# Scheduling by engine clocks, low parts inside P, and a two-pass V in a fused attention and feed-forward kernel

## The chip, the cores and the metric

The kernel runs on one core of a Trainium2 chip. The metric is device time in microseconds (us) of one execution; lower is better. Engines are named as in the profile: PE (TensorE, matrix products), DVE (VectorE), ACT (ScalarE, Exp and Tanh), POOL (GpSimd) and SP (SyncE, which issues most transfers).

## The reference

Multi-query attention (32 heads of 16, one shared K and V) and a SiLU feed-forward block on the same 2048 x 512 input, mixed per row by a sigmoid gate. All in fp32.

```python
def _A_ref(x, wq, wk, wv, wo):                   # S = 2048, D = 512, H = 32, Dh = 16
    q = (x @ wq) -> heads;  k = x @ wk;  v = x @ wv
    p = softmax(einsum("bhqd,bkd->bhqk", q, k) * Dh ** -0.5)
    return einsum("bhqk,bkd->bhqd", p, v) -> rows @ wo
def _B_ref(x, w1, w2):                           # F = 1792
    return silu(x @ w1) @ w2
g = sigmoid((x * gate_w).sum(-1))
out = g * _A_ref(x) + (1 - g) * _B_ref(x)
```

## The kernel before

**Precision.** An fp32 operand is written as two fp16 parts, high and low, and a product is three fp16 products (high by high, high by low, low by high). Only P V is different, see below.

**A prologue** (up to some 39 us) loads and transposes x, makes K and V of all keys, and the queries of the first heads. V lies as VF (fp32), VH and VL (its fp16 high and low parts), per block of 128 keys a tile of 16 columns of V and a 17th of ones, which gives the row sums of P, padded to 32 columns. `v_parts` makes VH and VL.

**The loop** of `attention` goes over 32 rounds (4 chunks of 512 rows, 4 groups of 8 heads, two halves `rb`) of 16 steps (blocks of 128 keys). A step has two score groups. Everything PE does is cut into *slots*: eight matmuls on 64 x 32 (or 50 x 32) tiles of the array, 512 columns each, which run side by side.

- `scores(p)`: one slot gives a 128 x 1024 score tile S in PSUM (two such tiles), then one Exp on ACT writes half of a step's P (128 x 2048, fp32, four buffers). 1024 of these.
- `pv(s, n)`: P V of a step adds into two PSUM banks that collect a round. A *native* step multiplies fp32 P by VF: eight fp32 matmuls, which take four slots of time. A *split* step uses the upper 16 bits of P as bf16 (`upper`, every other half word) and the rest as fp16: `low` subtracts the upper half from P on DVE, in two operations of 1024 elements, into a tile L of its own. Then three slots: VH by upper, VL by upper, VH by L. Odd steps are native, even ones split unless `split_step` says otherwise. The first matmul of a step needs the Exps; only the third slot needs L.
- the *stream* (`outs`, `stream`): the products of the feed-forward block, the query projection and the output projection, each an `Out` with 6 or 12 terms. A stream slot holds a term of one output on the upper 64 rows of the array and a term of the output before it on the lower 64. `ffn_h` evicts with Tanh on ACT, a gate product on DVE (L790) and a split of H into two fp16 parts on DVE (`split_v`, L120 and L121); `ffn_o` and `out_proj` add into the output rows on DVE (`add_out`, L720 and L722); `q_block` writes queries out to DRAM. PSUM has two banks (`pm`) for the stream.
- closing a round (`norm_a`, L943 to L950): two transposes out of PSUM, a sum over 17 of every 32 columns, reciprocal and product; every second round a transpose and a split (`norm_b`, `norm_c`) that give O for the output projection.
- splitting raw weights (`Pieces.step`, 36 pieces, loaded through POOL's queue) and the maxima for a range check (`chores`) fill DVE.

**What sets the order.** It is written out by hand: two steps form a cycle, and a string gives its slots, S for scores, F stream, P split slot, N native step, B a bound for the queries. Longer strings take over when the stream is behind. DVE's optional work goes through `put` and `fill`, which fills a cycle up to an assumed length (3.7, 4.1 or 4.95 us).

```python
SPLIT, NATIVE = "SFFFSFFFSPPPSBN", "SFFFSFFFSNBSN"
            fill(4.95 if n_f > 6 else 4.1 if ended[0] and ended[0].hidden else 3.7)
```

When the scores are through, the stream's remaining outputs are made as *whole* products (`whole`, 128 x 128 x 512, one slot each), in order.

**Range check.** Maxima are compared with `RANGES` at the end; outside them, a second, slower pass with measured scales runs (`second_pass`). Both passes call `attention`.

## Time and profile before

| | us |
|---|---|
| median of 3 runs | 1079.93 |
| fastest | 1078.13 |
| slowest | 1380.04 |
| span of the profiled execution (first to last instruction) | 1075.3 |
| first Exp of the loop starts | 39.3 |
| last Exp of the loop starts | 1053.0 |
| granted TensorE clock, mean over the span | 0.998 of full |

The profiled execution's own time is not listed beyond its span; what lies around the span is the difference to the times above. In the views, busy time is the union of an engine's records, a duration in ns is the mean of one instruction, "x8" counts instructions merged into a row, "PEld" is the loading of weights into the array, and `out<-in` names what an instruction writes and reads. A "chain" view follows the last instruction back through what released it. A few per cent of the matmul records are missing from the trace, so a row of 24 may show as x23.

### The profile page before, as it was taken

Reading aid. Unit: us, or ns where it says so; the run is one execution under the profiler, and the core shown is the slowest. Engines: PE = TensorE matmul, PEld = TensorE weight load, DVE = VectorE, ACT = ScalarE, POOL = GpSimd, SP = SyncE. Lnnn points to the kernel's source line nnn. Section 1 sums busy time; section 2 is a strip of 40 time slices with the busy share of each in tenths; the row PEclk is TensorE's granted clock in tenths of the full one; section 3 lists DMA queues with packets and bytes.
Section 4 is the critical chain, followed back from the end, with each engine's and each line's share of the span. In section 5 each row is a group of like instructions: output and inputs, shape, how many; then the busy total and the mean of one; then the engine's idle time right before and its main releaser. Section 6 shows DMA issues by size and latency. Waiting matters only on the chain.

```text
span 1075.3 us, 65967 instructions
## 1 busy us (share of the span) xinstructions
PE 1057.2 (98%) x31224; PEld 667.5 (62%) x31224; DVE 789.9 (73%) x1082; ACT 1008.6 (94%) x1121; POOL 23.4 (2%) x53
## 2 busy tenths in 40 slices
PE   8999999999999999999999999999999999999996
PEld 5455776766665577677655568677756555555552
DVE  6856986968778786878777697675857767476875
ACT  5799999999999999999999999899989999999992
POOL 2110000000000000000000000000000000000000
PEclk9999999999999999999999999999999999999999
DMA  5311111220001000000000100000000110000001
GB/s 208 115 61 45 49 42 31 61 60 14 11 11 41 32 22 10 17 12 12 22 11 21 37 19 21 22 12 11 20 6 12 31 31 12 11 11 5 11 4 43
DMA packets 20840, 32.95 MB, mean 31 GB/s; under 512 B 5137, under 2 KB 12050, under 8 KB 20562
## 3 DMA queue, kind: packets, MB, share of 16 engines
q1 hardware_dynamic: 17618, 20.46, 5.9%
q0 software_dynamic: 2512, 8.13, 2.6%
q8 instruction: 246, 4.03, 1.5%
q14 instruction: 32, 0.26, 0.1%
q10 hardware_dynamic: 432, 0.07, 0.0%
HBM read 20.12 MB, written 8.52 MB: 27 GB/s over the span
## 4 chain that ended last, share of the span: by engine, by line
PE 89%; DVE 5%; ACT 4%; issue 1%; POOL 0%; POOLq 0%; ACTq 0%
PE pv L1043 35%; PE pm L741 31%; PE S L997 19%; ACT P L1000 4%; DVE L L1021 1%; PE pm L745 1%; PE pt L311 0%; PE pk L126 0%; DVE xs L117 0%; DVE T L943 0%; PE pk L127 0%; PE pk L125 0%; DVE U L944 0%; PE pm L342 0%; DVE T L945 0%
## 5 line engine op out<-in xcount | busy, mean ns | idle before, releaser
L1000 ACT ACTIVATE P<-S 128x1024 f32<-128x1024 f32 x1024 | 963.5, 1051 | 24.6 <-PE S L997 19.4
L997 PE MATMUL S<-qb,KT 50*32 50x512 f16 x8192 | 480.1, 378 | 2.3 <-ACT P L1000 2.2
L1021 DVE TENSOR_TENSOR L<-P 128x1024 f16<-128x1024 f32 x348 | 408.1, 1217 | 8.3 <-ACT P L1000 8.2
L1043 PE MATMUL pv<-P,VF 64*32 64x512 f32 x5408 | 374.8, 589 | 0.0
L997 PEld LDWEIGHTS <-KT 50*32 50x32 f16 x8192 | 188.6, 90 | 193.9 <-issue 126.7
L741 PE MATMUL pm<-w2s,H 64*32 64x512 f16 x5232 | 258.8, 375 | 0.6 <-DVE qx L825 0.2
L741 PE MATMUL pm<-xs,w1s 64*32 64x512 f16 x5376 | 248.5, 375 | 1.1 <-issue 0.6
L741 PEld LDWEIGHTS <-H 64*32 64x32 f16 x5232 | 143.7, 93 | 43.5 <-issue 11.3
L741 PEld LDWEIGHTS <-w1s 64*32 64x32 f16 x5376 | 136.3, 93 | 46.1 <-issue 13.5
L1043 PEld LDWEIGHTS pv<-P,VF 64*32 64x32 f32 x5408 | 125.0, 107 | 30.3 <-issue 8.1
L790 DVE SCALAR_TENSOR_TENSOR e<-e,pm 128x512 f32<-128x512 f32 x56 | 38.5, 687 | 140.3 <-ACT e L789 139.4
L1043 PE MATMUL pv<-P,VH 64*32 64x512 bf16 x1392 | 81.9, 389 | 0.0
L1043 PE MATMUL pv<-L,VH 64*32 64x512 f16 x1392 | 81.4, 374 | 0.0
L1043 PE MATMUL pv<-P,VL 64*32 64x512 bf16 x1392 | 81.4, 385 | 0.0
L741 PE MATMUL pm<-xs,wqs 64*32 64x512 f16 x1152 | 81.1, 375 | 0.0
L1043 PEld LDWEIGHTS <-VH 64*32 64x32 f16 x2784 | 60.7, 92 | 20.4 <-issue 3.8
L741 PE MATMUL pm<-wo_s,O 64*32 64x512 f16 x1440 | 63.3, 375 | 0.0
L943 DVE STREAM_TRANSPOSE T<-pv 128x512 f32<-128x512 f32 x32 | 23.0, 717 | 48.0 <-PE pv L1043 40.4
L722 DVE SCALAR_TENSOR_TENSOR acc<-pm,g,acc 128x512 f32<-128x512 f32 x48 | 35.8, 745 | 26.4 <-PE pm L741 24.6
L741 PEld LDWEIGHTS <-wqs 64*32 64x32 f16 x1152 | 43.6, 93 | 10.1 <-issue 2.8
L121 DVE TENSOR_TENSOR H<-e,H 128x512 f16<-128x512 f32 x56 | 38.8, 693 | 1.9
L789 ACT ACTIVATE e<-pm 128x512 f32<-128x512 f32 x56 | 34.5, 616 | 5.7 <-PE pm L741 5.7
(155 smaller groups left out, 478.9 us busy)
## 6 DMA issues: line engine op xcount, KB each, us to landing
qb<-qd SPq DMA_DIRECT2D x192, 32.0 KB
raw<-in_B_w_dram POOLq DMA_DIRECT2D x23, 256.0 KB, 2.9
xn<-in_A_x_dram SPq DMA_DIRECT2D x8, 512.0 KB
out_dram<-acc SPq DMA_DIRECT2D x16, 256.0 KB
qd<-qx SPq DMA_DIRECT2D x12, 256.0 KB
raw<-in_A_wo_dram POOLq DMA_DIRECT2D x4, 256.0 KB, 3.6
qb<-sh SPq DMA_DIRECT2D x62, 2.0 KB
raw<-in_B_w_dram SPq DMA_DIRECT2D x3, 256.0 KB
```

The source lines that it names most:

```text
L121: nc.vector.tensor_tensor(a2, a, a1, op=OP.subtract)
L722: nc.vector.scalar_tensor_tensor(a, po, gate[:, n:n + 1], a, op0=OP.mult, op1=OP.add)
L741: nc.tensor.matmul(self.bank[32 * m:32 * m + 32], l(i, rows, 32 * m), r(j, rows), start=first, stop=last)
L745: nc.tensor.matmul(self.bank, l(i, slice(0, 128), 0, 128), r(j, slice(0, 128)), start=first, stop=last)
L789: nc.scalar.activation(e, ph, AF.Tanh, scale=t_scale)
L790: nc.vector.scalar_tensor_tensor(e, e, 1.0, ph, op0=OP.add, op1=OP.mult)
L943: nc.vector.transpose(T, pv[0])
L997: nc.tensor.matmul(sc[32 * m:32 * m + 32, f], KT[b:b + 50, k0:k0 + 32], qtile[i][b:b + 50, j], start=True, stop=True)
L1000: nc.scalar.activation(P[:, 2 * j:2 * j + 2], sc, AF.Exp, scale=scale_of(c, o))
L1021: nc.vector.tensor_tensor(lows[s][:, q], P[:, q], upper(P)[:, q], op=OP.subtract)
L1043: nc.tensor.matmul(pvs[i][h][32 * j:32 * j + 32], a[r], b[r, j], start=first, stop=last)
```

## The change

The strings and the cycle filler go. The program now keeps three clocks while it writes instructions out, `pe`, `act` and `dve`, with a fixed duration for each kind of work, and picks the next slot by them: a score when the one before the last should be through Exp, else stream or P V as far as they are ready by the clocks. DVE's operations become tasks with a duration, a time from which they are ready and a due time; `serve` issues them up to PE's clock.

- *Low parts in place*: `low` is one DVE operation over the whole step (2048 elements). It writes fp16 into the lower half words of P itself. L goes; P has five buffers instead of four.
- *Two-pass V*: VH and VL become one tile VP, whose 32 columns hold the high parts of V (0 to 15), the ones (16) and the low parts of columns 1 to 15 (17 to 31). A split step is two slots, VP by upper (U) and VP by low (L). There is no room for the low part of column 0, so the high parts of columns 0 to 6 lie on a coarse grid and the low parts of 1 to 6 carry one base-4 digit each of column 0's rest (`v_parts`, some 27 small DVE operations in the prologue, with the multipliers `mu`). Closing a round adds low to high columns and collects the digits (`joined`).
- *Native steps* are two units of 256 columns each ("a", "b"), except where one opens a round. An even step becomes native when the order reaches it with room and its low part is not yet issued (`make_native`).
- *U waits*: both slots of a split step are placed after the low part's end by DVE's clock (`can_go`).
- *H's split* goes from DVE to POOL.
- *Range*: V's largest magnitude must lie in 512 to 8000 instead of 1 to 6e4.

In the built program, before and after: split steps 174 and 218, native 338 and 294; stream slots in all 1660 and 1572; whole products 54 and 144, of which after the last score 30 and 120. The number of Exps (1024), Tanhs (56) and transfers of data is the same.

```diff
-SPLIT, NATIVE = "SFFFSFFFSPPPSBN", "SFFFSFFFSNBSN"
+SLOT, LOW = 0.2165, 2.3
+LATER, HURRY, PIECE, PB = 0.2, 4, 5.6, 5
...
-    VH = consts.tile([128, NKT, 32], F16)
-    VL = consts.tile([128, NKT, 32], F16)
+    VP = consts.tile([128, NKT, 32], F16)
...
+        def choice():
+            now = dve[0]
+            open_ = [t for t in tasks if t[1] <= now]
+            if not open_:
+                return None
+            t = min(open_, key=lambda t: t[0])
+            for u in tasks:
+                if u[4] and now < u[1] < now + t[2] and now + t[2] + u[2] > u[0] + 0.6:
...
+        def serve(until):
+            while dve[0] < until:
+                t = choice()
+                if t:
+                    do(t)
+                else:
+                    dve[0] = min([t[1] for t in tasks] + [until])
...
             def evict(ph):
                 e = wp.tile([128, 512], F32, name="e", bufs=2)
                 nc.scalar.activation(e, ph, AF.Tanh, scale=t_scale)
-                nc.vector.scalar_tensor_tensor(e, e, 1.0, ph, op0=OP.add, op1=OP.mult)
-                H = Hs[k, f] = wp.tile([128, 2, 512], F16, name="H", bufs=2 * NF)
-                spend(0.62)
-                put(1.0, 2, lambda: split_v(H[:, 0], H[:, 1], e))
+                begin = max(act[0], pe[0] + 0.2)
+                act[0] = begin + 0.46
+                def gate():
+                    nc.vector.scalar_tensor_tensor(e, e, 1.0, ph, op0=OP.add, op1=OP.mult)
+                    H = Hs[k, f] = wp.tile([128, 2, 512], F16, name="H", bufs=2 * NF)
+                    nc.gpsimd.tensor_copy(H[:, 0], e)
+                    nc.gpsimd.tensor_tensor(H[:, 1], e, H[:, 0], op=OP.subtract)
+                return put(0.68, begin + 0.62, begin + 0.7, gate, True)
...
+            def joined():
+                z = wp.tile([128, 16, 1 + DIGITS], F32, name="z")
+                nc.vector.tensor_tensor(z[:, :, 1:], T3[:, :, 17:17 + DIGITS], mu[:, :, 1:].to_broadcast([128, 16, DIGITS]), op=OP.mult)
+                nc.vector.tensor_tensor(T3[:, :, 1:16], T3[:, :, 1:16], T3[:, :, 17:32], op=OP.add)
+                nc.vector.tensor_reduce(z[:, :, 0:1], z[:, :, 1:], axis=AX.X, op=OP.add)
+                nc.vector.tensor_tensor(T3[:, :, 0:1], T3[:, :, 0:1], z[:, :, 0:1], op=OP.add)
...
-            nc.vector.tensor_tensor(lows[s][:, q], P[:, q], upper(P)[:, q], op=OP.subtract)
+            nc.vector.tensor_tensor(half(P, F16, 0), P, half(P, BF, 1), op=OP.subtract)
+            low_end[s] = dve[0] + 0.06
...
+        def can_go(s):
+            i = steps[s][0]
+            if not units_of(s) or ends.get(2 * s + 1, 1e9) + 0.05 > pe[0]:
+                return False
+            if i and i not in opened and not closed_by(i - 1):
+                return False
+            return s % 2 or s in native or low_end.get(s, 1e9) <= pe[0]
...
+        while p < n_s:
+            serve(pe[0])
+            due = ends.get(p - 2, 0.0) + 0.05
+            room = due + LATER - pe[0]
...
+            if n is not None and behind >= HURRY:
+                sums(n)
+            elif room >= SLOT and f_ready():
+                f_slot()
+            elif n is not None:
+                sums(n)
+            else:
...
+                if k is not None and room >= 2 * SLOT:
+                    make_native(k)
+                elif room >= SLOT and pe[0] + 0.02 < due:
+                    pe[0] += 0.05
+                else:
+                    scores(p)
+                    p += 1
```

More of the change, by code (lines that the diff above doesn't have):

```diff
@@ L976, in prefetch @@
                     load_q(qtile[i], c, o, rb, shifts)
[L979 to L985 removed]
+        probs, ends, low_end, lows = {}, {}, {}, {}
+        qtile = {}
         def scores(p):
@@ new lines, in cost, with whole_step, make_native, waiting @@
+        def cost(s):
+            return SLOT if units_of(s)[0] in "UL" else 2 * SLOT if steps[s][0] in opened else 4 * SLOT
+        def whole_step(s):
+            return lows.get(s) in tasks and units_of(s) == ["U", "L"]
+        def make_native(s):
+            native.add(s)
+            units[s] = ["a", "b"]
+            tasks.remove(lows[s])
+        def waiting():
+            s0 = first[0]
+            return range(s0, min((s0 // NKT + 1) * NKT, scored[0] // 2))
+        def sums_next(room):
+            return next((s for s in waiting() if can_go(s) and cost(s) <= room + (0 if units_of(s)[0] in "UL" else 0.1)), None)
@@ L1113 @@
+        while True:
+            while tasks:
+                do(min(tasks, key=lambda t: t[0]))
+            o = ahead.pop() if ahead else fetch()
+            if o is None:
+                break
+            for n in range(o.n):
+                o.whole(n, n == 0, n == o.n - 1)
+            force(o.evict(o.bank))
     with tc.manual_schedule():
```

574 lines of the change are left out of this document (332 added, 242 removed).

## The prediction

> **What bounds the kernel now.** I read the page's busy line first, then the share of the chain of waits, then that chain in the middle of the run. They give one picture.
>
> ```profile
> span 1075.3 us, 65967 instructions
> PE 1057.2 (98%) x31224; PEld 667.5 (62%) x31224; DVE 789.9 (73%) x1082; ACT 1008.6 (94%) x1121; POOL 23.4 (2%) x53
> PE 89%; DVE 5%; ACT 4%; issue 1%; POOL 0%; POOLq 0%; ACTq 0%
> ...
> 503.45 0.86 PE pv L1043 x16
> 504.31 0.22 PE S L997 x8
> 504.53 0.65 PE pm L741 x24
> ...
> 506.27 0.68 PE pv L1043 x23
> ```
>
> The chain is PE with no gaps: a slot of eight scores takes 0.22 us, three slots of stream 0.65 (0.217 each), one native P V step 0.86 (four slots), one split step 0.68 (three). So in the attention loop time is slots times 0.217. ACT is the runner-up at 94%, and how near it is has to be read from its pace, as its records overlap:
>
> ```profile
> L1000 ACT ACTIVATE P<-S x1024: 1016/1033/1187, 39.3 to 1053.0; 128x1024 f32<-128x1024 f32 x171
> 942.61 1.02 ACT L1000 ACTIVATE P<-S 128x1024 f32<-128x1024 f32 x1
> 943.51 0.60 ACT L789 ACTIVATE e<-pm 128x512 f32<-128x512 f32 x1
> 943.99 4.71 ACT L1000 ACTIVATE P<-S 128x1024 f32<-128x1024 f32 x5
> 1029.12 25.07 ACT L1000 ACTIVATE P<-S 128x1024 f32<-128x1024 f32 x27
> ```
>
> An Exp lasts 1.02 us but the next instruction starts 0.90 after it; a Tanh holds ACT for 0.48; five Exps in 4.71 less the last one's 1.1 give 0.905 each. ACT therefore can't do the loop under 1024 x 0.905 + 56 x 0.48 = 954 us. It took from 39.3 to 1054.2 (1029.12 + 25.07), 1014.9. So PE may give back about 60 us before ACT takes over; that is the ceiling for everything below.
>
> **PE's slots.** I counted the built programs' orders between the first and the last score. Before: 1654 stream slots, 1024 scores, 173 split steps at 3, 336 native steps at 4, 14 whole products: 4555 slots, 987 us at 0.2167. The trace took 1013.6 for it (scores from 38.8 to 1052.4), 2.7% more. After: 1561 stream slots, 1024 scores, 432 slots of split P V (two per step), 1168 of native P V, 14 whole products: 4199, or 910 us. In the whole program native steps fall from 338 to 294 (-176 slots) and split ones rise from 174 to 218 but cost 2 for 3 (522 to 436, -86): P V loses 262 slots, 57 us. The rest of the difference is not removed: 93 stream slots leave the loop, and whole products after the last score grow from 30 to 120.
>
> Native steps are now two halves of 256 columns, each loading all its weights again. A half loads 16 tiles; its columns take half of 0.86, 0.43:
>
> ```profile
> 498.16 0.45 PEld L1043 LDWEIGHTS pv<-P,VF 64*32 64x32 f32 x16
> ```
>
> Loading is then the longer side by 0.02, times 580 halves: 12 us. It can't be below 0 (the columns must pass) and, if the loads hid not at all, 0.45 x 580 = 261 us; the row shows loads overlapping in every slot today, so I take 12. PE's loop is 922, with its own 2.7% 947: just under ACT's 954. **ACT becomes the bound**, with PE at 97% of it.
>
> **What ACT loses over its floor.** Per round of 32 Exps I took the larger of PE's count and ACT's floor: before, these sum to 994 and the trace took 1014.9, 2.0% more (ends of scores, banks, a slow start). In the new order ACT is the larger in 29 of 32 rounds, sum 954. PE has about 3% in hand in a mean round, so I take 1.7%, between 0.5% and 4%: 970 us.
>
> The slack behind this is small:
>
> ```profile
> 38.78 0.41 PE L997 MATMUL S<-qb,KT 50*32 50x512 f16 x8
> 39.26 1.94 ACT L1000 ACTIVATE P<-S 128x1024 f32<-128x1024 f32 x2 [1.20 <-PE S L997]
> ```
>
> Scores need 0.48 us before their Exp can start. With two score tiles, a score must start after the Exp two before it (1.02) and be ready at 2 x 0.90: 1.80 - 1.02 - 0.48 = 0.3 us in which PE may be late. This is also the price of the new wait: the first P V product of a split step used to need the Exp alone, now it needs the whole low part. Queued behind it on PE are the stream and the next score, and behind that score ACT. A low part that comes more than about 0.3 us later than the order supposes goes into the time.
>
> **VectorE.** Its durations, from the groups:
>
> ```profile
> L1021 DVE TENSOR_TENSOR L<-P 128x1024 f16<-128x1024 f32 x348 | 408.1, 1217 | 8.3 <-ACT P L1000 8.2
> L121 DVE TENSOR_TENSOR H<-e,H 128x512 f16<-128x512 f32 x56 | 38.8, 693 | 1.9
> L120 DVE CAST H<-e 128x512 f16<-128x512 f32 x56 | 23.7, 423 | 0.6
> L945 DVE TENSOR_TENSOR T<-T,U 128x272 f32<-128x272 f32 x32 | 14.2, 444 | 1.1
> L950 DVE TENSOR_TENSOR C<-T,rr 128x256 f32<-128x256 f32 x32 | 13.6, 425 | 1.1
> L947 DVE RECIPROCAL rr<-T 128x16 f32<-128x16 f32 x32 | 8.1, 254 | 1.1
> ```
>
> Low parts: 408.1/348 is 1.17 each back to back, 2.3 for one of 2048 elements; 218 of them are 501 us, +93. Two bounds, as no row shows a write into every other half word of the tile being read: 2.2 (less the fixed cost of one instruction) and 4.6 if such a write took two passes. [...] The stream's two H operations leave for POOL, -62.5. Closing a round: the sum grows from 272 to 512 columns (0.44 to 0.69) and four operations of 96, 240, 96 and 16 columns come, by the rows between 0.17 and 0.42, 1.1 together: 32 x 1.35 = 43. Together 790 + 93 - 63 + 43 + 5 for the V digits = 868, of which some 31 lie outside the loop:
>
> ```profile
> 0.00:20.00 20.00, 14.75 (x77) 10.38 (x78) 10.61 (x35) 9.21 (x17) 5.11 (x20) 1.00 0.79 279
> 20.00:40.00 20.00, 19.93 (x118) 9.48 (x117) 14.79 (x31) 14.33 (x26) 1.76 (x3) 1.00 0.25 79
> ```
>
> (VectorE's busy time is the third in each row: 10.6 and 14.8 ahead of the loop; some 6 are in the tail). 837 in 970 is 86%, but uneven: over some twelve rounds in which weights are still split and maxima taken, the order holds about 27 us of VectorE work per 30 us round, later 23. Covered, with little to spare in the first third.
>
> The digits' 25 small operations (0.17 to 0.42 each, some 5 us) stand in front of the first query eviction. Ten Exps can run on five P buffers before a P V must, so I charge them inside the 1.7%; uncovered they cost 5.
>
> **POOL.** 112 operations arrive there, queued with the 33 raw weight loads.
>
> ```profile
> L304 POOL COPY wkv<-wvr 128x64 f32<-128x64 f32 x1 | 0.2, 237 | 0.0
> L305 POOL COPY wkv<-gwr 128x4 f32<-128x4 f32 x1 | 0.2, 190 | 1.0 <-DMA gwr<-in_gate_w_dram 1.0
> L209 POOL MEMSET VF<- 128x512 f32 x1 | 0.5, 525 | 0.0
> ```
>
> 60 more columns cost 0.047, so a copy of 512 takes about 0.6; the two-input one lies between that and twice that. At most 1.8 x 56 = 101 us in 970, and H is read a block later: hidden. A load ahead of them in POOL's queue waits for VectorE's piece, which stands ahead of H's gate on VectorE as well, so that costs nothing new. [...]
>
> **The tail.** From the end of the last Exp to the end of the span is 21.1 us today.
>
> ```profile
> 1056.63 0.70 DVE T L943
> 1057.33 0.61 DVE U L944
> ...
> 1060.41 3.64 PE pm L745 x9
> 1064.05 0.03 issue
> 1064.08 0.81 PE pm L745 x3
> 1064.89 0.01 issue
> 1064.90 4.06 PE pm L745 x18
> 1068.95 0.02 issue
> 1068.98 0.75 DVE acc L722
> ```
>
> PE sits idle until the last closing is through, then does 12 products of `wo` at 0.37 and 18 at 0.226. After: the closing grows by 1.35 and one accumulate of 0.75 stands in it, +2; ninety whole products more at 0.2167 to 0.226, +20. Tail 43. None of it has cover, as ACT is done.
>
> **Sum.** 39.3 + 970 + 43 = 1052 us of span. Around the span lie 4.6 us to the median of 1079.93 and 2.8 to the fastest run; I add 4: **1056 us**.
>
> **Rivals.** (1) *ACT loses next to nothing*: an order that knows the engines' paces keeps it at its floor (0.5%, 959): 1041 of span, 1045. For it: in the row from 943.99 ACT held 0.905 with PE equally loaded. Against: the 27 Exps from 1029.12 took 0.92 each even with VectorE light. 0.08.
>
> [...] 0.24.
>
> (3) *Slower: the low parts cost more than 2.3.* VectorE has 837 in the loop and 218 of them; no change leaves a loop of 994 (1079.9 - 4 - 39.3 - 43), so it decides from 2.3 + (994 - 837)/218 = 3.0 us. At 3.2, VectorE takes 1033 and with the 86 around it the time is 1119; at the two-pass bound of 4.6, 1338 + 86 = 1424. For it: the write is new in kind. Against: the spacing is one the row already reads at. 0.12.
>
> (4) *It does not do what it says*: the forward pass hands over to the slow second pass when the largest |V| is outside the new 512 to 8000. With the reference's inputs it is 3601, so no second pass; under 0.01.
>
> **Chances and range.** The forecast (0.56) reaches from 1040 to 1070: its unknown losses (0.5 to 4% of ACT's floor is 23 us on both sides together, the halves 12, the start 5). 2% is 1058.3, about what a measurement of this kernel can tell from no change. Three quarters of the forecast and all of (1) lie below it: 0.50 faster. The other quarter and (2) are within 2%: 0.38. (3) gives 0.12 slower. Leaving out (3) and the ends of (1) and (2), the range is 1038 to 1084.
>
> **What would show it.** ACT: Exp to Exp 0.90 to 0.92 through the loop, the last Exp near 1009, and the chain split between PE and ACT where it was PE. PE: idle a few per cent before scores, waiting on Exp. L1152 near 2.3 us; over 3.0 it is rival 3. [...] Tail: about 120 whole products in 27 us. Wrong would be a loop that is longer with ACT waiting for scores that wait for nothing: PE's halves mis-sized.

## The result, and the profile after

| | median, us | runs from, to | ratio to the kernel before, 95% interval |
|---|---|---|---|
| kernel before, beside it | 1079.36 | 1078.13 to 1079.93, and one at 1380.04 | |
| changed kernel | 1093.77 | 1091.13 to 1095.22 | 1.0138 [1.0119, 1.0158] |
| changed kernel again, unedited, in a later session | 1078.47 | 1075.81 to 1085.46 | 1.001 [0.9994, 1.0026] |

The run at 1380.04 is a slow one, and the ratios are of fast runs alone.

The forecast was 1056 us, from 1038 to 1084. The recorded time lies outside it, on the other side of the kernel before. The last row comes from the end of the study, and it changed the explanation: the same program was 15 us quicker in a later session, while the kernel before stayed within two microseconds from session to session. The later session ran on chip 5; the chip of the first is not on record, so session and chip can't be told apart here. Both have to be explained: what ate the expected gain in either session, and what took 15 us more in the first.

The page of the changed kernel, in the recorded session: span, busy time, the chain's shares by engine, and the groups of the low part and of POOL's new work (busy us, mean ns; idle before).

```profile
span 1090.7 us, 71347 instructions
PE 1045.6 (96%) x33874; PEld 661.4 (61%) x33874; DVE 951.4 (87%) x994; ACT 1003.8 (92%) x1121; POOL 194.2 (18%) x170
...
PE 57%; DVE 18%; ACT 17%; issue 6%; DMA 1%; POOL 0%; ACTq 0%; POOLq 0%; DVEq 0%
...
L1152 DVE TENSOR_TENSOR P<-P 128x2048 f16<-128x2048 f32 x218 | 590.9, 2717 | 43.0 <-ACT P L1140 42.8
L829 POOL CAST H<-e 128x512 f16<-128x512 f32 x56 | 76.1, 1359 | 752.0 <-DVE e L827 751.8
L830 POOL TENSOR_TENSOR H<-e,H 128x512 f16<-128x512 f32 x56 | 95.3, 1701 | 4.5
```

TensorE had 98% of the kernel before and is still at 96%, though 262 slots of P V are gone; its products have even risen from 31,224 to 33,874. VectorE is at 951 us where the prediction had 868, the low part at 2.72 us where it had 2.3. The Exps, by their line (count, duration in ns min/median/max, first and last start):

```profile
L1140 ACT ACTIVATE P<-S x1024: 1011/1047/1259, 39.4 to 1046.1; 128x1024 f32<-128x1024 f32 x171
```

I call the time from the first Exp's start to the last one's end the loop, and what follows the tail. Before: 1014.9 and 21.1 us. Changed: 39.4 to 1047.2, 1007.8, and 43.5. So the loop fell by 7 us and the tail grew by 22. In the later session the page reads:

```profile
span 1074.3 us, 71347 instructions
PE 1030.5 (96%) x33874; PEld 654.9 (61%) x33874; DVE 951.3 (89%) x994; ACT 998.2 (93%) x1121; POOL 193.9 (18%) x170
...
PE 50%; DVE 26%; ACT 17%; issue 6%; DMA 1%; another core or an unknown queue 0%; POOL 0%; ACTq 0%; POOLq 0%; DVEq 0%
```

```profile
L1140 ACT ACTIVATE P<-S x1024: 1012/1065/1261, 39.3 to 1030.5; 128x1024 f32<-128x1024 f32 x171
```

VectorE's and POOL's work is the same to 0.3 us, and so is the tail (42.7). The loop is 992.3. TensorE's busy time fell by 15 us with the same products: in the first session something stretched it. (A stop of TensorE shorter than a product lasts, some 0.38 us, does not show as idle in its busy time.)

### What TensorE waited for in the recorded session

The waits of TensorE that the profile puts down to nothing it shows, in the recorded session and then in the later one (us in total, times, longest):

```profile
PE pm L808 <- issue: 4.4, 7, 2.4
PE S L1134 <- issue: 2.3, 4, 1.2
PE pv L1211 <- issue: 1.5, 4, 0.7
```

```profile
PE pm L808 <- issue: 2.1, 1, 2.1
PE S L1134 <- issue: 0.8, 2, 0.7
PE pv L1211 <- issue: 0.2, 1, 0.2
```

Lined up Exp by Exp, the two traces differ at many places by 0.3 to 0.8 us each, where ACT got its scores late in the recorded session only. The chain of waits shows what happens there (start, length, what):

```profile
731.15 0.22 PE S L1134 x6
731.37 0.14 PE pm L808
731.51 0.19 issue
731.71 0.84 PE pm L808 x23
...
735.15 0.22 PE S L1134 x8
735.37 0.07 PE pv L1211
735.43 0.29 issue
735.73 0.63 PE pv L1211 x11
```

TensorE stops between two products, once in the stream and once in P V, with nothing late: no semaphore ends the wait. The 16 KB packets of the program queue tell more. The stops end at 731.71 and 735.73; the next packets start at 732.85 and 736.88, 1.14 and 1.15 us later. So I took, in each trace, every pause of 0.3 to 1.5 us between starts on TensorE from 60 to 1000 us, and counted those whose end lies 0.9 to 1.5 us ahead of a program packet. Of random instants 16% lie there, which gives the share due to chance.

```
kernel                    packet   pauses     in step with   by
                          median   all, us    a packet, us   chance
before                     0.99    312 108.5   41  15.2      16.3
changed, recorded          1.02    122  63.0   48  23.9      10.1
changed, later session     0.96    108  58.6   21  11.5       9.4
```

Beyond chance that is 14 us in the recorded session, 2 in the later, none in the kernel before: 12 of the 15.5 us between the two loops. The difference depends on how one counts: with only the pauses that end 1.0 to 1.25 us ahead of a packet it is 16 and 6 us beyond chance, so 10 of the 15.5. 36 of the recorded trace's pauses lie in that narrow band. **So TensorE was most likely waiting for its own program**; no run changed the packets alone. The rates fit. A packet holds 16,384 bytes; in stretches where TensorE runs at 0.027 us a product, packets start 3.4 us apart (the shortest tenth, 3.43). The median spacing is 4.05 us in the kernel before and 3.76 in the changed one. From the stops: 1.1 us from a stop's end to the next packet's start, 0.96 or 1.02 us for a median packet, 1.4 from its end to the end of a stop. That is 3.5 us, as long as the spacing of packets at full pace, so by this reading slower packets can tip it over. Why a packet starts only 1.1 us after a stop's end no run shows. Why packets were slower in that session isn't known; later sessions had both kinds, and chip 8 alone had medians from 0.96 to 1.01 us.

The change had raised the density. A native step of 0.86 us was 16 records on TensorE before (the rows of the prediction's first fence); now its half is:

```profile
732.76 0.43 PE pv L1211 x16
```

P V went from 338 x 16 + 174 x 24 = 9,584 records to 12,864 (32 for a native step, 16 for the two that open a round undivided and for each of the 218 split ones), each with a weight load, in 57 us less of TensorE's time by the count of slots. The half lasts what its columns last, half of 0.86.

### The profile page after: what moved, and what is told of

Its sections match the earlier page's. It is cut to its first block, busy times and chain, and to the rows that moved or that the text cites. A ratio compares the mean times of both kernels' runs of the same rounds, so it can differ in the third digit from the quotient of the medians.

```text
span 1090.7 us, 71347 instructions
## 1 busy us (share of the span) xinstructions
PE 1045.6 (96%) x33874; PEld 661.4 (61%) x33874; DVE 951.4 (87%) x994; ACT 1003.8 (92%) x1121; POOL 194.2 (18%) x170
## 4 chain that ended last, share of the span: by engine, by line
PE 57%; DVE 18%; ACT 17%; issue 6%; DMA 1%; POOL 0%; ACTq 0%; POOLq 0%; DVEq 0%
PE pv L1211 20%; PE pm L808 20%; ACT P L1140 16%; PE S L1134 13%; DVE P L1152 10%; PE pm L812 3%; ACT e L822 1%; DVE e L827 1%; DVE acc L783 1%; DVE mxs L137 1%; DVE T L1064 0%; DVE C L1086 0%; DMA gwr<-in_gate_w_dram 0%; DVE U L1065 0%; DVE O L123 0%
## 5 line engine op out<-in xcount | busy, mean ns | idle before, releaser
L1152 DVE TENSOR_TENSOR P<-P 128x2048 f16<-128x2048 f32 x218 | 590.9, 2717 | 43.0 <-ACT P L1140 42.8
L1134 PE MATMUL S<-qb,KT 50*32 50x512 f16 x8192 | 508.5, 380 | 10.1 <-ACT P L1140 6.5
L1211 PE MATMUL pv<-P,VF 64*32 64x256 f32 (+1 forms) x9376 | 385.3, 378 | 1.3 <-issue 0.8
L1211 PEld LDWEIGHTS pv<-P,VF 64*32 64x32 f32 x9376 | 205.8, 106 | 66.1 <-issue 12.3
L829 POOL CAST H<-e 128x512 f16<-128x512 f32 x56 | 76.1, 1359 | 752.0 <-DVE e L827 751.8
L1211 PE MATMUL pv<-P,VP 64*32 64x512 f16 (+1 forms) x3488 | 180.5, 389 | 4.2 <-DVE P L1152 2.6
L808 PEld LDWEIGHTS <-H 64*32 64x32 f16 x4704 | 117.9, 93 | 46.4 <-issue 10.4
L1211 PEld LDWEIGHTS <-VP 64*32 64x32 f16 x3488 | 75.0, 92 | 39.6 <-issue 16.8
L830 POOL TENSOR_TENSOR H<-e,H 128x512 f16<-128x512 f32 x56 | 95.3, 1701 | 4.5
L827 DVE SCALAR_TENSOR_TENSOR e<-e,pm 128x512 f32<-128x512 f32 x56 | 38.2, 683 | 28.0 <-ACT e L822 27.8
L808 PEld LDWEIGHTS <-O 64*32 64x32 f16 x1440 | 32.7, 92 | 14.7 <-issue 3.6
L180 POOL DMA_DIRECT2D raw<-in_B_w_dram x27 | 14.9, 553 | 110.1 <-DVE w1s L198 62.6
```

The source lines that it names most:

```text
L180: queue.dma_start(r, src)
L808: nc.tensor.matmul(self.bank[32 * m:32 * m + 32], l(i, rows, 32 * m), r(j, rows), start=first, stop=last)
L827: nc.vector.scalar_tensor_tensor(e, e, 1.0, ph, op0=OP.add, op1=OP.mult)
L829: nc.gpsimd.tensor_copy(H[:, 0], e)
L830: nc.gpsimd.tensor_tensor(H[:, 1], e, H[:, 0], op=OP.subtract)
L1134: nc.tensor.matmul(sc[32 * m:32 * m + 32, f], KT[b:b + 50, k0:k0 + 32], qtile[i][b:b + 50, j], start=True, stop=True)
```

## The experiments

All in one table; loop, tail and packets are those of the profiled run. The chance share of the pauses is in brackets.

```
                              median    ratio [95%]               loop   tail  packet  in step
low part cut                  1070.94   0.9912 [0.9879, 0.9944]   987.3  42.6   0.96   13.9 ( 7.5)
H's low part left out         1073.70   0.995  [0.9931, 0.997]    990.9  43.1   0.96   13.1 ( 8.4)
both                          1071.77   0.9933 [0.9916, 0.9949]   987.1  42.5   0.96   14.4 ( 7.3)
low part's clock 2.7          1089.31   1.0081 [1.0053, 1.0108]   987.0  62.6   0.96   10.8 (10.9)
four buffers, low in place    1107.78   1.0286 [1.0257, 1.0315]  1012.3  52.8   0.99   22.6 (12.3)
four buffers, low apart       1093.29   1.0148 [1.0116, 1.018]    998.6  52.4   0.97   23.4 (12.0)
two-pass V alone              1085.03   1.0066 [1.005, 1.0083]   1019.7  22.6   1.01   21.3 (24.3)
clocks 0.930 and 2.5          1069.67   0.9923 [0.991, 0.9935]   1005.3  21.9   0.96   15.7 ( 8.1)
  the same, later             1071.03   0.9935 [0.9922, 0.9947]  1005.9  21.7   0.96   19.2 ( 8.0)
digits late                   1084.89   1.0061 [1.0048, 1.0074]   999.5  42.1   0.96   16.0 (11.1)
clocks and digits             1079.43   1.0012 [1.0003, 1.0022]  1007.5  27.8   0.96   17.9 ( 8.8)
clocks 0.945 and 2.7          1089.98   1.0112 [1.0061, 1.0164]  1029.0  19.7   1.00   24.1 (10.0)
Exp's clock 0.915 alone       1093.43   1.013  [1.0108, 1.0152]  1019.9  29.9   1.00   30.3 (11.0)
0.930 and 2.5, cut            1083.86   1.0048 [1.0025, 1.0071]  1023.7  22.3   1.01   34.1 (10.2)
0.945 and 2.7, cut            1084.09   1.0063 [1.0038, 1.0088]  1020.6  19.8   0.98   26.1 ( 9.1)
0.915, cut                    1081.24   1.0007 [0.9977, 1.0036]  1014.5  31.1   1.02   37.0 (10.3)
```

Packets came at 0.96 us or near 1.0. The first seven rows ran on chip 8 (the first four in one session, the next three in another), the two-clock and digit rows and the later session of the changed kernel on chip 5, the last five on chip 6. Where two kernels are compared below, I say whether both had the same packets; that leaves the chips as a difference.

**VectorE relieved: the low part cut, H's low part left out, both.**

```diff
-            nc.vector.tensor_tensor(half(P, F16, 0), P, half(P, BF, 1), op=OP.subtract)
+            nc.vector.tensor_tensor(half(P, F16, 0)[:, :, 0:440], P[:, :, 0:440], half(P, BF, 1)[:, :, 0:440], op=OP.subtract)
```

```diff
-                    nc.vector.scalar_tensor_tensor(e, e, 1.0, ph, op0=OP.add, op1=OP.mult)
                     H = Hs[k, f] = wp.tile([128, 2, 512], F16, name="H", bufs=2 * NF)
-                    nc.gpsimd.tensor_copy(H[:, 0], e)
-                    nc.gpsimd.tensor_tensor(H[:, 1], e, H[:, 0], op=OP.subtract)
+                    nc.vector.scalar_tensor_tensor(H[:, 0], e, 1.0, ph, op0=OP.add, op1=OP.mult)
```

In the first the product with the low part takes 440 columns as well. In the second the feed-forward product's third term reads the high part of H in place of the low one. Both leave out a part of the result and serve only to measure.

> The order of instructions is that of the changed kernel. The low part covers 440 of the 512 columns of each head pair, and the second slot of a split step reads only those 440 (the low part of the other 72 columns is left out), so that one low part should last near the 2.3 us that the order's clock gives it, not the 2.66 that it lasted undisturbed in the changed kernel. Theory A (the low part is longer than the order supposes: 218 x 0.36 = 78 us of VectorE work that the order does not know of): the loop from the first Exp to the end of the last falls from 1007.8 to 970 to 985, the time to 1056 to 1070. Theory B (POOL's reads hold VectorE up: 29 us of longer VectorE instructions beside POOL's): VectorE has 78 us to spare, but the late bursts stay; 1080 to 1090. Theory C (the order itself, slots and Exps, costs the 54 us over ACT's floor): 1088 to 1094.

> The gate writes H's high part directly, POOL's two operations per H go, and the low part of H is left out (the third term reads the high part). PE, ACT and the number of VectorE instructions stay. A: VectorE gets 29 us back of some 107 too much, 1080 to 1088. B: the loop loses most of what it has over its floor, 1056 to 1070, and VectorE's two-input instructions all have the durations that they have without POOL beside them (L1086 near 425 ns, L1152 near 2660). C: 1088 to 1094.

> Both edits: the low part at 440 columns and no POOL operations, with the low parts that the two leave out left out here as well. A and B together: VectorE is then at the prices that the forecast gave it, and the time should be the forecast's 1056, 1048 to 1064. If A alone: as the cut low part alone, within 3 us. If C: 1085 or more, and what is left over ACT's floor is PE's and ACT's own.

The loops are 987.3, 990.9 and 987.1. When only the recorded 1007.8 stood beside them, this looked like 17 to 20 us of VectorE's excess. Against the later session, which had the same packets (0.96), it is 992.3: 5, 1.4 and 5 us. With the pauses beyond chance taken off (2 there; 6, 5 and 7 here) 990 stands against 981, 986 and 980. So VectorE's excess costs 4 to 10 us by these runs, and the two reliefs don't add. The expectations were reckoned from 1007.8: the first run came out just above theory A's ranges, the second between A's and B's, and the third within 3 us of the first, as 'A alone' had it. With POOL's operations gone, VectorE's two-input operations go back to their length (O's low part, L123, from 924 ns to 692); the closing's product, in the changed kernel and without POOL's work (mean ns after the bar):

```profile
L1086 DVE TENSOR_TENSOR C<-T,rr 128x256 f32<-128x256 f32 x32 | 18.9, 592 | 1.1
```

```profile
L1084 DVE TENSOR_TENSOR C<-T,rr 128x256 f32<-128x256 f32 x32 | 13.6, 425 | 1.1
```

Summed over every VectorE operation that ran beside POOL's, it was 29 us in the changed kernel; of the low parts, 169 with no POOL beside them took 2.66 us and 49 with it 2.91.

**The low part's clock.**

```diff
-SLOT, LOW = 0.2165, 2.3
+SLOT, LOW = 0.2165, 2.7
```

> Only the clock's constant for a low part goes from 2.3 to 2.7; everything is computed. The order changes: 202 split steps for 218, 310 native for 294, and whole products after the last score go from 120 to 204, 84 x 0.22 = 18 us of tail. A: the loop gets 30 to 45 us shorter as nothing comes late, less 7 for 32 more slots of native P V on PE that is not the bound; with the tail 1065 to 1085. B: the loop falls by 5 to 10 only, and the tail takes more than that: 1095 to 1105. C: 1105 to 1112 (the tail alone).

The order gives up 16 split steps and leaves 204 whole products for the tail instead of 120. The loop is 987.0, 5 us less than the changed kernel's with equal packets; the tail is 62.6, 20 more, and the time is longer: this order moves work behind the last Exp, where nothing covers it. The time lies between the ranges of theories A and B, and none of the three foresaw it.

**Four buffers, the low part in place or in its own tile, in the same order.**

```diff
-            nc.vector.tensor_tensor(half(P, F16, 0), P, half(P, BF, 1), op=OP.subtract)
+            Ls[s] = wp.tile([128, 4, 512], F16, name="L", bufs=2)
+            nc.vector.tensor_tensor(Ls[s], P, half(P, BF, 1), op=OP.subtract)
```

> The changed kernel with four P buffers in place of five, low parts still in P's own halves. The order changes a little: 228 split steps (218), 284 native, 156 whole products after the last score (120, so 8 us more tail). It is the twin of the next run. Theory A+B (VectorE over its limit, by the length of the low part and by POOL's reads; either alone is enough to bring the stalls): 10 more low parts at 2.66 are 27 us more VectorE, loop 1010 to 1025, time 1100 to 1120. If five buffers were what the loop lived on, over 1120. Theory C (VectorE does not matter): loop 1008, time 1100.

> The same order of instructions as its twin, and all is computed, but each low part goes into a tile of its own, in consecutive half words (two such tiles). A: the 2.66 us come from the write into every other half word, so one low part falls to 2.2 to 2.35 us undisturbed (the kernel before: two of half the size in 2.35), VectorE gets some 75 us back, and the loop falls to 987, where it ended in the three runs that relieved VectorE; with a tail of about 50 the time is 1074 to 1082. If the length came from reading P beside ACT's writes, or from the single long operation, it stays at 2.66 and the time at that of its twin.

```profile
L1152 DVE TENSOR_TENSOR P<-P 128x2048 f16<-128x2048 f32 x228 | 619.7, 2724 | 32.5 <-ACT P L1140 32.3
```

```profile
L1153 DVE TENSOR_TENSOR L<-P 128x2048 f16<-128x2048 f32 x228 | 535.2, 2349 | 50.7 <-ACT P L1140 50.2
```

One pair, one session, the same pauses in step with packets (10 and 11 beyond chance): 85 us less of low parts (VectorE's busy time falls by 70, from 974.9 to 904.8) and 13.7 us less of loop. This is the cleanest measure of the low part's price, in an order with four buffers; five buffers with a tile of its own were not run. The first kernel came as theory A+B had it. In the second the low part took 2.28 us with no POOL operation beside it, as expected, but the loop stayed 11 us above the expected 987 and the time 11 us above its range.

**Two-pass V alone, in the order written out by hand.**

```diff
-SPLIT, NATIVE = "SFFFSFFFSPPPSBN", "SFFFSFFFSNBSN"
+SPLIT, NATIVE = "SFFFSFFFSPPSBN", "SFFFSFFFSNBSN"
```

> The kernel before with the two-pass V alone: its hand-written order less one P slot, low parts in their own tile in two operations, four P buffers, H split on VectorE; V in the two-in-one form, the longer closing of a round, the V digits in the prologue. 174 slots of P V go (4602 to 4428, 37.7 us of PE), nothing moves into the tail (30 whole products). VectorE: 790 + 43 + 5 = 838. If the loss of the changed kernel lies in VectorE's overload and in the tail, this keeps most of the PE gain: the loop falls from 1015 to ACT's floor of 954 plus the 36 that the runs without VectorE's overload kept, 985 to 995, tail 23, time 1050 to 1065. If the hand-written order can't use free slots (ACT idle as before, cycles as long as before), 1070 to 1080.

174 slots fewer and 1019.7 us of loop, 5 more than before. A split cycle of 16 slots is now 3.47 us, under ACT's 3.62 for four Exps, so by this count ACT sets its pace; the native cycles of 18 and the wide ones keep TensorE as the bound, and nothing moves work from one to the other. The time lies above both expected ranges. The 5 us more of loop are about two stops of ACT: 2.7 us at 47 us, behind the digits of V, and 3.2 us at 803 us, where the kernel before has one of 1.5. Apart from such stops the rounds take as long as before, so in this order the free slots brought nothing.

**The order's clocks told what the chip took.**

```diff
-SLOT, LOW = 0.2165, 2.3
+SLOT, LOW = 0.2165, 2.5
-            act[0] = begin + 0.902
-            ends[p] = begin + 1.018
+            act[0] = begin + 0.93
+            ends[p] = begin + 1.046
```

> Edit: only the order's clocks: an Exp is booked at 0.930 us instead of 0.902 (the loop of the relieved kernels ran 987 us against 954 of ACT's own work, that is 0.93 for each Exp), a low part at 2.5 instead of 2.3. The order then leaves 24 whole products for the tail instead of 120, with 293 split steps turned whole against 294: 96 slots (20.8 us of TensorE) move from the tail into the loop. Theory (in the loop of the changed kernel TensorE has slots to spare that the order's fast clock did not use): the loop stays at 1000 to 1010 us, the tail falls to about 22, the time to 1066 to 1074, below the kernel before (ratio 0.988 to 0.995). Rival (the loop is short of TensorE as well): it grows by the 20.8 us that the tail loses, and the time stays at 1090 to 1095.

```profile
L1140 ACT ACTIVATE P<-S x1024: 1014/1032/1160, 39.4 to 1043.6; 128x1024 f32<-128x1024 f32 x171
```

The numbers came as expected, for a reason that holds only in part. Against the changed kernel's later run, with the same packets, the loop grew by 13 us for 20.8 us of slots moved in, and the tail fell by 21: by that, a third of the moved work was free. It is the fastest full version here.

**The digits of V behind the first query evictions**, alone and with those clocks. The recorded trace has the chain from 35.94 us (VP, L341) to 42.29 (L357), 6.35 us, ahead of the first query eviction. The wait it causes, on TensorE and then on ACT:

```profile
44.85 0.39 PE L365 MATMUL pm<-qx,kab 64*32 64x512 f16 x2 [2.06 <-DVE O L902]
```

```profile
47.24 1.94 ACT L1140 ACTIVATE P<-S 128x1024 f32<-128x1024 f32 x2 [3.36 <-PE S L1134]
```

```diff
-            v_parts(sb)
             note()
...
         def low(s):
+            if digits:
+                T = wp.tile([128, 512], F32, name="T")
+                digits.pop()(T)
+                dve[0] += 6.0
```

> Edit: the chain of small VectorE operations that makes the digits of V (6.35 us in the trace of the changed kernel) is issued ahead of the first low part, behind the first stretch's query evictions, and the order's clock is told 6.0 us for it; 120 whole products in the tail as in the changed kernel. Theory (the 3.4 us that ACT loses at 47 us come from the first query eviction, held by this chain): the first stretch's loss goes, 1089 to 1091 us. Rival (the chain only moves to where VectorE is the tighter engine): the 6 us come back in the first rounds, 1093 to 1097.

> Edit: the two together (Exp booked at 0.930, low part at 2.5, the digits of V ahead of the first low part). The order leaves 48 whole products in the tail here, 24 more than with the clocks alone (5.2 us of TensorE). If the late digits save 3.4 us and the slots in the loop are free: tail about 27, loop 997 to 1007, 1066 to 1074 us, level with the clocks alone. If the digits cost in the loop what they save ahead of it: 5 us above the clocks alone.

ACT in the late version, and the chain there:

```profile
44.37 12.94 ACT L1143 ACTIVATE P<-S 128x1024 f32<-128x1024 f32 x14 [0.49 <-PE S L1137]
61.84 1.94 ACT L1143 ACTIVATE P<-S 128x1024 f32<-128x1024 f32 x2 [4.52 <-PE S L1137]
```

```profile
57.82 0.12 DVE VP L361
57.95 0.05 issue
57.99 2.62 DVE P L1159
60.61 0.04 issue
60.65 0.63 PE pv L1218 x8
61.28 0.85 PE S L1137 x16
```

The 3.36 us at 47 is gone and 4.52 come at 62: the first low part now stands behind the digits, and the first split P V behind that. Neither number of the first expectation is met, as both started from 1093.8; against 1078.5 with the same packets it is 6 us slower. The rival was right that the digits come back where VectorE is tighter, but not all of the 6 us is theirs: another stop of ACT, 4.0 us at 217, is in this trace and not in the changed kernel's. There a cast of H on POOL lasted 7.4 us from 199.8, the load of a raw weight that stands behind it in POOL's queue landed late, and VectorE waited for it:

```profile
211.63 0.43 DVE L197 TENSOR_SCALAR wo_s<-raw 128x512 f16<-128x512 f32 x1 [4.30 <-DMA raw<-in_A_wo_dram]
```

With the clocks the late digits are 8 to 10 us slower than the clocks alone, more than the 5 expected; 6 of that is tail (27.8 for 21.9) and 2 loop.

**The clocks pushed further, and the Exp's clock alone.**

```diff
-SLOT, LOW = 0.2165, 2.3
+SLOT, LOW = 0.2165, 2.7
-            act[0] = begin + 0.902
+            act[0] = begin + 0.945
```

> Edit: the order's clocks further up: 0.945 us for an Exp, 2.7 for a low part (the 2.66 measured). 308 steps whole (294 in the changed kernel), 18 whole products in the tail (120): 102 slots more in the loop than in the changed kernel, 186 more than with the low part's clock alone, which had a loop of 987 us and a tail of 62.6. Theory (what the loop needs beyond ACT's own work is idle TensorE, and VectorE's excess costs the rest): VectorE relieved as with the low part's clock alone, tail about 21, and of the 186 slots (40.3 us) the idle part of TensorE in the 987 us takes about half: loop 1000 to 1010, 1060 to 1070 us, level with or below the two clocks before. Rival (with VectorE relieved TensorE is the bound again, and each slot put back costs its 0.2165 us): loop 1027, 1087 us.

> Edit: the Exp's clock alone, 0.915 us for 0.902; the low part stays booked at 2.3. 60 whole products in the tail for 120, 292 steps whole for 294. Theory (VectorE's excess holds the loop at 1000 to 1010 us, and TensorE has idle slots in it): the tail loses 60 x 0.2165 = 13 us, the loop stays: 1078 to 1084 us. Rival (what made the two clocks together faster was the low part's clock): loop 1014 to 1021, 1090 to 1094 us.

Both theories fell, and both loops and times came near the rivals' numbers. The chain's shares, first with both clocks further up, then with the Exp's alone:

```profile
PE 73%; ACT 11%; DVE 9%; issue 4%; POOL 1%; DMA 1%; ACTq 0%; POOLq 0%
```

```profile
PE 51%; DVE 28%; ACT 13%; issue 6%; DMA 1%; POOL 0%; ACTq 0%; POOLq 0%
```

With 102 slots more the chain is mostly TensorE's; with the low part booked too short VectorE has three times the share. Both ran in a session with slow packets (14 and 19 us of pauses beyond chance), so how much of the 1029 and 1020 is the order's own isn't known. In the second one, a program packet from 774.6 us took 5.5 us, and ACT stood ("remote" is a releaser that the records don't name):

```profile
782.05 2.20 ACT L1140 ACTIVATE P<-S 128x1024 f32<-128x1024 f32 x2 [4.82 <-remote]
```

Every whole kernel's trace has such a stop of 1.4 to 4.9 us somewhere between 764 and 803 us, behind a program packet of 2.1 to 5.5 us. The kernel before has it too: 1.5 us at 792.9, behind a packet of 3.1 us from 787.1. So the change did not bring it, but its length differs from trace to trace.

**The low part cut in those three orders**, with the edit of the first experiment.

> The order with both clocks (0.930 and 2.5), and the low part of 440 of 512 columns only, as in the first experiment: this leaves out the low part of 72 columns of each head, and takes 0.39 us of VectorE and 0.03 us of TensorE off each split step. 219 split steps: VectorE loses some 85 us of work, TensorE 6.7. If VectorE's excess still holds this loop (1005 us), it falls to 985 to 992; if TensorE holds it, it falls by no more than 7, to 998 to 1003.

> The order with the slower clocks (0.945 and 2.7), and the same cut (72 of 512 columns of the low part left out). If TensorE holds its loop (1029 us; TensorE has 73% of the chain of waits, the low part 4%), the cut gives no more than the 6.3 us that it takes off TensorE: 1022 to 1029. If VectorE holds it: below 1015.

> The order with the Exp's clock alone (0.915), and the same cut (72 of 512 columns of the low part left out). If VectorE holds its loop (1020 us; the low part has 17% of the chain of waits), it falls by 17 us or more as in the first experiment, to 995 to 1003; if TensorE holds it, by no more than 7, to 1013 to 1020.

The first is the run that upset the story: 76 us less of VectorE's work, and 14 us slower than the order with all of it (1083.9 against 1069.7), on another chip and with slower packets. Both of its expected loops were below 1005; it took 1023.7. Its chain:

```profile
PE 77%; ACT 13%; issue 5%; DVE 4%; DMA 0%; POOL 0%; ACTq 0%; POOLq 0%
```

Of its pauses 24 us beyond chance are in step with packets, against 8: that is 16 of the 18 us between the loops. The second lost 8.4 us of loop, about what is taken off TensorE, which fits TensorE as the bound of that order. The third is open: its runs spread from 1071.6 to 1093.9.

**The changed kernel and the two clocks again, unedited, on one chip.**

> The changed kernel once more, unedited, on one chip with the order of both clocks, since the last three kernels, which only leave work out of orders that ran before, ran on another chip than those, and one of them (two clocks and cut, 1083.9 us) was slower than the order with all its work (1069.7). If the loops differ by the order and its VectorE work, this one stays at 1091 to 1096 us here too. If the chip makes the difference (TensorE's waits for nothing shown are 8 to 15 us in the five kernels of that chip, 2 to 7 in nine of the other chips' runs), it may come anywhere from 1075 to 1095, and the order with two clocks moves with it.

> The order with both clocks (0.930 and 2.5) once more, unedited, beside the changed kernel. If its gain is the order's: 1067 to 1073 us, and 20 us or more below the changed kernel on the same chip. If it was the chip's: 1080 to 1090 us here, or level with the changed kernel.

The changed kernel moved by 15 us and the order with the two clocks, whose two runs were on the same chip, by 1. Neither expectation held as a whole: the changed kernel came out where a chip or a session makes the difference, and the two clocks did not move with it. On one chip in one session the clocks are worth 7.4 us, not 20: 0.9935 [0.9922, 0.9947] against 1.001 [0.9994, 1.0026].

**Single forms**, with all the rest left out.

```diff
+    for _ in range(12):
+        nc.vector.tensor_tensor(half(P, F16, 0), P, half(P, BF, 1), op=OP.subtract)
+    for _ in range(12):
+        nc.vector.tensor_tensor(half(Q, F16, 0), P, half(P, BF, 1), op=OP.subtract)
+    for _ in range(12):
+        nc.vector.tensor_tensor(L, P, half(P, BF, 1), op=OP.subtract)
...
+    for _ in range(40):
+        nc.gpsimd.tensor_tensor(G[:, 1], e, H[:, 0], op=OP.subtract)
```

> No attention at all: this kernel leaves out everything but a load, a store and series of single operations, to measure three forms of the low part (2,048 differences of a value and its upper half) by themselves: into the value's own lower half words, into the lower half words of another tile, and into consecutive half words; then the same beside an unbroken series of 512-element copies on POOL, then beside an unbroken series of 512-element subtractions on POOL; with them the two-input addition of 512 elements. If the stride of what is written makes the price, both strided forms take 2.66 us and the consecutive one 2.28; if working in place makes it, the strided form into another tile takes 2.28. If only POOL's two-input operation holds VectorE, the forms stretch beside the subtractions alone; if any POOL operation does, beside the copies too.

Alone: in place (L87), into another tile's half words (L89), consecutive (L91), the addition (L93):

```profile
L87 DVE TENSOR_TENSOR P<-P 128x2048 f16<-128x2048 f32 x12 | 29.0, 2419 | 0.0
L89 DVE TENSOR_TENSOR Q<-P 128x2048 f16<-128x2048 f32 x12 | 29.0, 2419 | 0.0
L91 DVE TENSOR_TENSOR L<-P 128x2048 f16<-128x2048 f32 x12 | 27.4, 2280 | 0.0
L93 DVE TENSOR_TENSOR T<-T,U 128x512 f32<-128x512 f32 x12 | 8.2, 680 | 0.0
```

The stride makes the price, not the place: 0.14 us alone. In the kernel it is 0.38 (2.66 against 2.28); that the engines around add the other 0.24 is only argued.

On the chip the series beside POOL did not run in the order of the program's text, so what ran beside what is read from the timeline. From 154.80 to 182.07 us POOL made 16 copies, one beside each of 16 operations of VectorE: a cast, two consecutive low parts (L104), six low parts in place (L112) and seven additions (L106). The subtractions on POOL had only the last consecutive low part (L114) and twelve additions (L116) beside them.

```profile
154.80 27.27 POOL L100 CAST G<-e 128x512 f16<-128x512 f32 x16
155.62 2.69 DVE L104 TENSOR_TENSOR L<-P 128x2048 f16<-128x2048 f32 x1
158.23 1.09 DVE L106 TENSOR_TENSOR T<-T,U 128x512 f32<-128x512 f32 x1
L112 DVE TENSOR_TENSOR P<-P 128x2048 f16<-128x2048 f32 x6 | 16.9, 2824 | 0.0
...
199.19 3.24 DVE L114 TENSOR_TENSOR L<-P 128x2048 f16<-128x2048 f32 x1
L116 DVE TENSOR_TENSOR T<-T,U 128x512 f32<-128x512 f32 x12 | 18.4, 1533 | 0.4
```

So a copy on POOL is enough to stretch VectorE: each of the three forms took 0.40 us more beside one (2.69 for 2.28, 2.82 for 2.42, 1.09 for 0.68). Beside a two-input subtraction it was 0.85 to 0.96 us more. POOL loses too:

```profile
L100 POOL CAST G<-e x60: 616/617/26387, 98.7 to 181.1; 128x512 f16<-128x512 f32 x60
```

A copy takes 0.62 us alone and 1.7 in that stretch, and the first one stood for 26.4 us under an unbroken series on VectorE.

## Why the prediction was wrong, step by step

The step that failed is "What ACT loses over its floor". The forecast's sum had 39.3 us ahead of the loop, 970 of loop and 43 of tail; 39.4, 1007.8 and 43.5 were measured, so all of the miss is in the loop. Its loss over the floor of 954 was taken as 1.7%, 16 us, and measured 54 (5.6%) in the recorded session and 38 (4.0%) in the later one.

- **ACT becomes the bound, loop 970.** The pace behind the floor held: after half of all Exps the next operation of ACT starts within 0.907 us, in both sessions. The loss above it was mis-sized. In the later session: 4 to 10 us from VectorE by the runs that relieve it, 3 at the start from the digits, 3 at the stop near 785, 2 to 6 of pauses in step with packets; some 20 us are left. Sorted by what TensorE did just ahead of each Exp that came over 0.06 us late, 13 us, in 84 such delays, come where pauses of TensorE of 0.3 us or more don't make up half of the delay: it was mostly busy with other slots. Another 7 us are delays of under 0.06 us each. The same sorting gives VectorE 13 us. It is an estimate, and no run separates these parts. The recorded session adds 10 to 12 us of pauses in step with packets and 3 to 5 that aren't placed.
- **P V's slots, 262 fewer, 57 us.** Right as a count of TensorE's time. The halves were charged 12 us for their weight loads, and a half took its columns' 0.43, so that term was not needed. What the prediction left out is the number of instructions: fewer slots with more of them (9,584 records of P V before, 12,864 after), and, by the reading above, a program that comes hardly faster than it is used (3.5 us from stop to stop, packets 3.4 us apart at full pace). None of the rivals was about it. The last sentence of the prediction names the sign ("a loop that is longer with ACT waiting for scores that wait for nothing") but puts it down to the halves' size.
- **The low part, 2.3 us.** That was twice the 1.17 us of a row that writes consecutive half words; alone the consecutive form took 2.28 and the strided one 2.42. In the kernel it took 2.66, inside the bounds and under rival 3's point of 3.0; with POOL beside it 2.91. VectorE came to 951 for 868. TensorE waited for low parts 7 times in the recorded session, 2.6 us in all, and 5.8 us in the later one; the slack of 0.3 us at this wait was not measured by itself.
- **POOL hidden; the chance of 0.24 for (2).** POOL's durations were right (medians of 0.61 and 1.17 us). VectorE's operations were longer beside POOL's, 29 us in all, and POOL stood as well: its copies took 1.36 us in the mean, its subtractions 1.70. Among the single forms it was 0.40 us more beside a copy and 0.85 to 0.96 beside a subtraction. All this is worth some 4 us of time (one run, on another chip), and no run shows it holding the loop, which is what the 0.24 stood for. The prediction had no term for a load that stands behind H's operations in POOL's queue; in the run with the late digits one such load cost ACT 4 us.
- **The digits, about 5 us, covered.** They took 6.35 and weren't covered: the bound product (L365) waits for the eviction that stands behind them on VectorE, and the next scores are queued behind that product on TensorE, so the ten Exps didn't get theirs.
- **The tail, 43 us.** 43.5 and 42.7. Right, and it took back 22 of what the loop gave.
- **Rivals 1 and 4** didn't happen.

So the 57 us went like this. Of 1014.9 us of loop 22.6 came off in the later session, as ACT's floor and the losses above it stop it there; the tail took 21.6 back. The recorded session lost 15 more, some 10 to 12 of them in step with the program's packets.

## What to carry to other kernels

Time taken off an engine must be counted with its instructions: here TensorE did small products at 0.027 us each, packets of its program started 3.4 us apart, and columns were saved while products rose from 31,224 to 33,874; part of the gain most likely went into waits that no semaphore shows (2 to 14 us of 57). Where two engines are both near their limits, the loss above the slower one's floor needs terms of its own; here it was the whole miss. The clocks of a planner have to be measured in the kernel and not taken from an operation by itself (a low part took 2.42 us alone and 2.66 here), and the work left for the tail has to be read beside the loop. A difference of one or two per cent between two versions needs both on one chip in one session, since a kernel that stands still from session to session does not vouch for its successor.

## What the runs showed of the hardware

The program's 16 KB packets took 0.96 us in some sessions and near 1.0 in others, and the dense orders lost from nothing to 27 us of pauses in step with them, where the kernel before lost none at 0.99. Single packets took 2.1 to 5.5 us, and ACT stood for 1.4 to 4.9 us behind them, in the kernel before as well. Writing 2,048 half words at a stride of two costs 2.42 us against 2.28 alone, and 2.66 against 2.28 beside the rest of this kernel. An unbroken series on VectorE held a 512-element copy on POOL for 26.4 us. Beside one copy on POOL a two-input operation of VectorE took 0.40 us more, and beside a series of subtractions a VectorE addition of 512 took 1.53 us for 0.68.
